# Order and bank flags of the output products in a decay attention with a feed-forward behind it

## The chip, the cores and the metric

The kernel runs on one core of a Trainium2 chip. The metric is the time of one execution on the device in microseconds (us). A core has five engines that run side by side and wait for each other by semaphores: TensorE (PE in the profile) multiplies matrices and writes into eight accumulator banks (PSUM), VectorE (DVE) and ScalarE (ACT) read those banks, GpSimd (POOL) works on the main on-chip memory alone, and SyncE (SP) issues the transfers.

## The reference

Eight heads of decayed linear attention over 4 batches of 768 tokens with head size 64, then a feed-forward layer with softplus:

```python
for t in range(S):
    state = gamma[None, :, None, None] * state + np.einsum('bhd,bhe->bhde', k[:, :, t], v[:, :, t])
    y[:, :, t] = scale * np.einsum('bhd,bhde->bhe', q[:, :, t], state)
...
x = np.ascontiguousarray(attn_out.transpose(0, 2, 1, 3)).reshape(B * S, H * D)
h = x @ w_in
g = np.maximum(h, 0.0) + np.log1p(np.exp(-np.abs(h)))
return (g @ w_out).astype(np.float32)
```

Here gamma differs by head; w_in is 512 by 2048, w_out 2048 by 512.

## The kernel before, in words

**Attention in units.** A unit is one chunk of 128 tokens for half of the heads (four heads): 4 batches of 6 chunks and 2 halves make 48. A unit passes through parts, one every few ticks: its loads (`load_unit`), the decay factors (`decay`, POOL), the operands (`operands`), the scores (`scores`), the new state (`new_state`), and the outputs with a copy of the state (`stack_and_outputs`). The state of earlier chunks stays summed in one bank (`stp`).

**Split operands.** PE multiplies in a reduced format (fp32r). The later units, those from number 12 on (WHOLE), therefore hold each operand as a high part and a low part: `kq` for keys and queries, `vhl` for values, `st` for the state, `ah` and `al` for the masked scores. Scores are made by PE two heads at a time (`sc`, L227), added up by DVE (L228), masked by POOL (L229), cast to `ah` by ACT (L233), and `al` is the difference, made by POOL (L234).

**The outputs.** For a later unit the outputs of its four heads lie in one tile `yp` of 64 partitions and 512 numbers, which fills one bank. Per head five products are summed there: state with the queries' high and low parts (L298, L299; not in a batch's first chunk, where there is no state), values' high part with `ah` (L300), values' high part with `al` (L301), values' low part with `ah` (L302). Then ACT casts them to `xh` (L304) and DVE takes the rest, `xl` (L306). Scores and outputs share the two banks of the pool `ps_a`.

**The feed-forward.** Blocks of 256 or 384 tokens go through 16 slices of the hidden size. A step makes one slice `hp` from `xh`, `xl` and the split first weights (L334 to L336, two banks in turn), then softplus in three steps on DVE and ACT (L341, L342, L346), a cast to `gh` (L348, ACT) and a rest `gl` (L350, POOL); two steps later the second product adds into `acc` (L365 to L367).

**What sets the order.** The code issues attention ticks between feed-forward steps by a plan. The order in which each engine then has its instructions comes from a scheduler that runs through the program with a modelled timeline: where an instruction's inputs are not there yet in its model, it puts a later instruction of the same engine that is ready ahead of it, and it picks the buffers of a pool along the way. On the chip every engine goes through its list strictly in that order.

Of the kernel before, what the change touches and what calls it, by code (L numbers as in the profile page):

```python
# [33 lines left out]
def decay_attention_then_softplus_ffn(ctx: ExitStack, tc: tile.TileContext, q, k, v, w_in, w_out, qtab, vtab, gtab, out):  # L34
    nc = tc.nc
# [8 lines left out]
    HH = H // 2  # L44
# [228 lines left out]
    def outputs(n):  # L273
        b, c, hf = units[n]
        kq, *rest, st = live.pop(n)
        off, g = places[n // 2], hf * NJ
        xh, xl = (x[:, g:g + NJ, off:off + C] for x in xring)
        if n < WHOLE:
            kn, vn, a = rest
            yp = ps_a.tile([P, NJ, C], F32, name="yp", tag="a")  # L280
            v0 = vns[n % 3].rearrange("p h t d -> p (h t) d")
            for j in range(NJ):
                if c:
                    nc.tensor.matmul(yp[:, j], lhsT=st[:, j, :], rhs=kq[:, j, :], start=True, stop=False)
                for par in range(2):
                    at = 2 * (2 * j + par) - par
                    nc.tensor.matmul(yp[:, j], lhsT=v0[:, at:at + 2, :], rhs=a[:, 2 * j + par, :], start=c == 0 and par == 0, stop=par == 1)
            nc.scalar.copy(xh, yp)
            nc.vector.tensor_tensor(xl, yp, xh.bitcast(F32), op=ALU.subtract)
            return  # L290
        yp = ps_a.tile([D, 2, NJ, C], F32, name="yp", tag="a")
        vhl, kn, vn, ah, al = rest
        for j in range(NJ):
            for par in range(2):
                h = 2 * j + par
                o = yp[:, par, j, :]
                if c:
                    nc.tensor.matmul(o, lhsT=st[:, par, j, :], rhs=kq[:, 1, par, j, :], start=True, stop=False)  # L298
                    nc.tensor.matmul(o, lhsT=st[:, par, j, :], rhs=kq[:, 2, par, j, :], start=False, stop=False)  # L299
                nc.tensor.matmul(o, lhsT=vhl[:, h, 0, :], rhs=ah[:, h, :], start=c == 0, stop=False)  # L300
                nc.tensor.matmul(o, lhsT=vhl[:, h, 0, :], rhs=al[:, h, :], start=False, stop=False)  # L301
                nc.tensor.matmul(o, lhsT=vhl[:, h, 1, :], rhs=ah[:, h, :], start=False, stop=True)  # L302
        for par, own, oth in sides:
            nc.scalar.copy(xh[own], yp[:, par])  # L304
        for par, own, oth in sides:
            nc.vector.tensor_tensor(xl[own], yp[:, par], xh[own].bitcast(F32), op=ALU.subtract)  # L306

    def stack_and_outputs(n):
        outputs(n)
        stack_state(n)  # L310
# [77 lines left out]
    for i, a, b in turns:  # L388
        m = WIDE // BLOCKS[i]
# [71 lines left out]
    for a, b in zip(starts, starts[1:]):  # L461
# [4 lines left out]
        for s in range(a, b):  # L466

            t, n = (s - a + 1, b - a) if i == 2 else (min(s - a, b - a - 2), b - a - 2)
# [59 lines left out]
```

## Time and profile before

| | |
|---|---|
| median of 3 runs | 686.2 us (682.22 to 686.45) |
| profiled execution | 683.14 us |
| its span, first to last instruction | 681.3 us |
| PE busy | 661.6 us (97%) |
| weight loads (PEld) busy | 600.3 us (88%) |
| DVE, ACT, POOL busy | 436.1, 358.0, 316.5 us |
| granted clock of PE | 0.997 |

Durations are those of the profiled execution. PE's matmuls overlap each other: one is shown from its start to its modelled end, and the next starts long before that end, so what a matmul costs in a dense stream is the step from start to start. Weight loads have rows of their own (PEld) and run beside the matmuls. A view that names a wait gives the idle time of an engine just before an instruction and what came last of that which it waited for.

### The profile page before, as it was taken

How to read it: one execution, taken by the hardware profiler on the slowest of the kernel's cores; microseconds unless marked ns; L12 is line 12 of the kernel's file. 1: busy time of each engine (PE TensorE's matmuls, PEld its weight loads, DVE VectorE, ACT ScalarE, POOL GpSimd, SP SyncE). 2: the span in 40 equal slices, each digit the busy share in tenths (PEclk: the TensorE clock that was granted, in tenths of full speed). 3: DMA queues.
4: the chain of work that ended last, by engine and by line, in shares of the span. 5: the costliest groups of instructions: out<-in, count | busy, mean ns of one | idle time of the engine just before them, and what ended most of it. 6: DMA issues, size and time to landing. Idle time of an engine off the chain costs nothing.

```text
span 681.3 us, 12857 instructions
## 1 busy us (share of the span) xinstructions
PE 661.6 (97%) x4146; PEld 600.3 (88%) x4146; DVE 436.1 (64%) x843; ACT 358.0 (53%) x808; POOL 316.5 (46%) x354
## 2 busy tenths in 40 slices
PE   7999899999999999999999999999999999999997
PEld 6898789988999999988999899988999899999996
DVE  5678698578567576785676766778666755432321
ACT  5788775545555355554555655455555545422221
POOL 5797666535435453454355344535344543332221
PEclk9999999999999999999999999999999999999999
DMA  9898653123112131222222222222212211000100
GB/s 246 237 270 231 184 141 72 26 69 82 35 36 53 29 95 26 40 39 64 48 38 54 37 77 42 37 36 53 76 37 38 36 33 47 1 1 1 46 1 32
DMA packets 153826, 46.75 MB, mean 69 GB/s; under 512 B 140448, under 2 KB 148640, under 8 KB 153760
## 3 DMA queue, kind: packets, MB, share of 16 engines
q1 hardware_dynamic: 153312, 45.93, 28.3%
q8 instruction: 33, 0.54, 0.3%
q14 instruction: 33, 0.27, 0.1%
q10 hardware_dynamic: 448, 0.01, 0.0%
HBM read 39.60 MB, written 6.29 MB: 67 GB/s over the span
## 4 chain that ended last, share of the span: by engine, by line
PE 52%; DVE 12%; SPq 11%; DMA 9%; issue 6%; ACT 5%; POOL 2%; DVEq 0%; ACTq 0%; POOLq 0%
SPq L136 10%; PE hp L334 8%; PE hp L336 8%; PE acc L365 8%; PE acc L367 8%; PE acc L366 8%; PE hp L335 8%; DVE kq L204 3%; DMA wout<-in_moe_w_out_dram 2%; DMA win<-in_moe_w_in_dram 2%; DMA kb<-in_k_dram 2%; DVE kq L208 2%; DMA qb<-in_q_dram 2%; DVE a L228 1%; DMA vn<-in_v_dram 1%
## 5 line engine op out<-in xcount | busy, mean ns | idle before, releaser
L350 POOL TENSOR_TENSOR gl<-sp,gh 128x384 fp32r<-128x384 f32 (+1 forms) x120 | 130.6, 1089 | 223.1 <-ACT gh L348 201.3
L334 PE MATMUL hp<-xh,winhl 128*128 128x384 f32 (+1 forms) x576 | 185.3, 322 | 2.4 <-DVE sp L346 1.9
L336 PE MATMUL hp<-xh,winhl 128*128 128x384 f32 (+1 forms) x576 | 184.7, 321 | 0.3 <-POOL winhl L99 0.3
L335 PE MATMUL hp<-xl,winhl 128*128 128x384 f32 (+1 forms) x576 | 183.7, 319 | 0.0
L365 PE MATMUL acc<-wouthl,gh 128*128 128x512 f32 x384 | 152.7, 398 | 0.0
L366 PE MATMUL acc<-wouthl,gh 128*128 128x512 f32 x384 | 151.8, 395 | 0.0
L367 PE MATMUL acc<-wouthl,gl 128*128 128x512 f32 x384 | 150.2, 395 | 0.0
L342 ACT ACTIVATE sp<-sp 128x384 f32<-128x384 f32 (+1 forms) x120 | 65.3, 546 | 137.7 <-DVE sp L341 134.6
L334 PEld LDWEIGHTS hp<-xh,winhl 128*128 128x128 f32 x576 | 108.8, 189 | 7.1 <-DVE sp L346 1.7
L335 PEld LDWEIGHTS hp<-xl,winhl 128*128 128x128 f32 x576 | 108.8, 189 | 3.7
L336 PEld LDWEIGHTS hp<-xh,winhl 128*128 128x128 f32 x576 | 108.7, 189 | 0.8 <-POOL winhl L99 0.5
L341 DVE TENSOR_SCALAR sp<-hp 128x384 uint32<-128x384 uint32 (+1 forms) x120 | 68.4, 573 | 61.1 <-PE hp L336 60.5
L348 ACT CAST gh<-sp 128x384 fp32r<-128x384 f32 (+1 forms) x120 | 64.1, 534 | 73.9 <-DVE sp L346 44.6
L346 DVE SCALAR_TENSOR_TENSOR sp<-hp,sp 128x384 f32<-128x384 f32 (+1 forms) x120 | 69.4, 580 | 34.6 <-ACT sp L342 33.6
L367 PEld LDWEIGHTS acc<-wouthl,gl 128*128 128x128 f32 x384 | 71.7, 188 | 14.4
L366 PEld LDWEIGHTS acc<-wouthl,gh 128*128 128x128 f32 x384 | 72.3, 188 | 11.1
L365 PEld LDWEIGHTS acc<-wouthl,gh 128*128 128x128 f32 x384 | 72.2, 188 | 10.9
L229 POOL TENSOR_SCALAR_AFFINE_SELECT a<-a 128x512 f32<-128x512 f32 x48 | 35.9, 749 | 48.5 <-DVE a L228 34.9
L228 DVE TENSOR_REDUCE a<-sc 128x256 f32<-128x512 f32 x72 | 48.9, 680 | 9.3 <-PE sc L227 7.8
L234 POOL TENSOR_TENSOR al<-a,ah 128x512 fp32r<-128x512 f32 x36 | 48.1, 1337 | 10.7 <-ACT ah L233 10.5
L204 DVE TENSOR_TENSOR kq<-kb,kq 64x256 fp32r<-64x256 f32 x72 | 49.7, 690 | 3.2 <-ACT kq L203 1.1
L199 DVE STREAM_TRANSPOSE kb<-kb 128x256 f32<-128x256 f32 x36 | 16.0, 445 | 51.8 <-DMA kb<-in_k_dram 39.8
(83 smaller groups left out, 994.0 us busy)
## 6 DMA issues: line engine op xcount, KB each, us to landing
win<-in_moe_w_in_dram SPq DMA_DIRECT2D x16, 512.0 KB, 4.5
wout<-in_moe_w_out_dram SPq DMA_DIRECT2D x16, 512.0 KB, 4.5
vn<-in_v_dram SPq DMA_DIRECT2D x48, 128.0 KB, 2.8
out_dram<-o SPq DMA_DIRECT2D x24, 256.0 KB, 2.1
kb<-in_k_dram SPq DMA_DIRECT2D x288, 16.0 KB, 1.7
qb<-in_q_dram SPq DMA_DIRECT2D x288, 16.0 KB, 1.7
vn<-in_k_dram SPq DMA_DIRECT2D x30, 128.0 KB, 2.4
qn<-in_q_dram SPq DMA_DIRECT2D x12, 128.0 KB, 4.7
```

The lines of the kernel that those rows point to most:

```text
L136: nc.sync.dma_start(t[at:at + 32, h // 2], src[b, hf * HH + h, c * C:(c + 1) * C, d:d + 32].rearrange("(i t) d -> t i d", t=32))
L204: nc.vector.tensor_tensor(kq[oth, 0, par], kt[own], kq[own, 0, par].bitcast(F32), op=ALU.subtract)
L334: nc.tensor.matmul(hp[:, k], lhsT=wt[:, 0, d, :], rhs=xh[:, d, :], start=d == 0, stop=False)
L335: nc.tensor.matmul(hp[:, k], lhsT=wt[:, 0, d, :], rhs=xl[:, d, :], start=False, stop=False)
L336: nc.tensor.matmul(hp[:, k], lhsT=wt[:, 1, d, :], rhs=xh[:, d, :], start=False, stop=d == ND - 1)
L341: nc.vector.tensor_scalar(sp.bitcast(U32), hps[s].bitcast(U32), 0x80000000, None, op0=ALU.bitwise_or)
L342: nc.scalar.activation(sp, sp, AF.Softplus)
L346: nc.vector.scalar_tensor_tensor(g, hps.pop(s), 0.0, g, op0=ALU.max, op1=ALU.add)
L350: nc.gpsimd.tensor_tensor(gl, sps.pop(s), gh.bitcast(F32), op=ALU.subtract)
L365: nc.tensor.matmul(acc[i][t], lhsT=gh[:, k, ts], rhs=wt[:, 0], start=begins and k == 0, stop=False)
L366: nc.tensor.matmul(acc[i][t], lhsT=gh[:, k, ts], rhs=wt[:, 1], start=False, stop=False)
L367: nc.tensor.matmul(acc[i][t], lhsT=gl[:, k, ts], rhs=wt[:, 0], start=False, stop=ends and f == fs[-1])
```

## The change

The products of a later unit's outputs are the same, in another order. Per head the new code issues the state products and the two products with `ah`; when all four heads have had theirs, it issues the four products with `al`. [...] Now only the very first matmul into the bank clears; all others add where something has been written since, and overwrite where nothing has. All have to come after that first one, which a dependency without a semaphore states.

```diff
--- before.py
+++ after.py
@@ -290,16 +290,27 @@
             return
         yp = ps_a.tile([D, 2, NJ, C], F32, name="yp", tag="a")
         vhl, kn, vn, ah, al = rest
+        opened = []
+
+
+        def into(o, l, r):
+            m = nc.tensor.matmul(o, lhsT=l, rhs=r, start=not opened, stop=True, skip_group_check=True)
+            if opened:
+                tc.add_manual_dep(m.ins, opened[0].name, mybir.DependencyInfo(mybir.DependencyClass.NoSync, mybir.DependencyReason.DATA), reason="the bank's first")
+            else:
+                opened.append(m.ins)
+
         for j in range(NJ):
             for par in range(2):
                 h = 2 * j + par
-                o = yp[:, par, j, :]
+                products = [(vhl[:, h, 0, :], ah[:, h, :]), (vhl[:, h, 1, :], ah[:, h, :])]
                 if c:
-                    nc.tensor.matmul(o, lhsT=st[:, par, j, :], rhs=kq[:, 1, par, j, :], start=True, stop=False)
-                    nc.tensor.matmul(o, lhsT=st[:, par, j, :], rhs=kq[:, 2, par, j, :], start=False, stop=False)
-                nc.tensor.matmul(o, lhsT=vhl[:, h, 0, :], rhs=ah[:, h, :], start=c == 0, stop=False)
-                nc.tensor.matmul(o, lhsT=vhl[:, h, 0, :], rhs=al[:, h, :], start=False, stop=False)
-                nc.tensor.matmul(o, lhsT=vhl[:, h, 1, :], rhs=ah[:, h, :], start=False, stop=True)
+                    products = [(st[:, par, j, :], kq[:, t, par, j, :]) for t in (1, 2)] + products
+                for l, r in products:
+                    into(yp[:, par, j, :], l, r)
+
+        for h in range(HH):
+            into(yp[:, h % 2, h // 2, :], vhl[:, h, 0, :], al[:, h, :])
         for par, own, oth in sides:
             nc.scalar.copy(xh[own], yp[:, par])
         for par, own, oth in sides:
```

In the new code all these products have one line, L297. Lines behind the change are numbered 11 higher than before (L334 is now L345, L341 is L352, L365 is L376).

PE, the run of the unit whose tile is `yp_4546`, from its first product with `ah`; `sc_4629` are the next unit's scores, `hp` and `acc` the feed-forward. Before:

```order
L227 MATMUL sc_4629<-kq1_85 128x256 x2
L300 MATMUL yp_4546<-ah_4474,vhl_4370 64x128
L365 MATMUL acc0_3971<-wouthl_901,gh_4495 128x512
L366 MATMUL acc0_3971<-wouthl_901,gh_4495 128x512
L367 MATMUL acc0_3971<-wouthl_901,gl_4497 128x512
L365 MATMUL acc1_3972<-wouthl_901,gh_4495 128x512
L366 MATMUL acc1_3972<-wouthl_901,gh_4495 128x512
L367 MATMUL acc1_3972<-wouthl_901,gl_4497 128x512
L365 MATMUL acc2_3973<-wouthl_901,gh_4495 128x512
L301 MATMUL yp_4546<-al_4475,vhl_4370 64x128
L302 MATMUL yp_4546<-ah_4474,vhl_4370 64x128
```

Now (the products of the last head with the state and `ah`, then what follows; those of the first three heads stand just ahead):

```order
L297 MATMUL yp_4546<-kq0_84,st0_4264 64x128 x2
L297 MATMUL yp_4546<-ah_4474,vhl_4370 64x128 x2
L297 MATMUL yp_4546<-al_4475,vhl_4370 64x128 x4
L346 MATMUL hp_4585<-xl_83,winhl_1122 128x384
L347 MATMUL hp_4585<-xh_82,winhl_1122 128x384
L345 MATMUL hp_4585<-xh_82,winhl_1122 128x384
L346 MATMUL hp_4585<-xl_83,winhl_1122 128x384
L347 MATMUL hp_4585<-xh_82,winhl_1122 128x384
L227 MATMUL sc_4629<-kq1_85 128x256 x2
```

Seven `acc` matmuls stood between the first product with `ah` and the first with `al`; now the other `yp` products stand there, and five `hp` matmuls and the next unit's scores, which were ahead of the run, come behind it.

PE, the unit `yp_3716` of a batch's first chunk (no state products). Before:

```order
L366 MATMUL acc0_3012<-wouthl_1131,gh_3620 128x512
L300 MATMUL yp_3716<-ah_3656,vhl_3548 64x128
L227 MATMUL sc_3782<-kq0_84 128x256 x2
L367 MATMUL acc0_3012<-wouthl_1131,gl_3622 128x512
L365 MATMUL acc1_3013<-wouthl_1131,gh_3620 128x512
L366 MATMUL acc1_3013<-wouthl_1131,gh_3620 128x512
L367 MATMUL acc1_3013<-wouthl_1131,gl_3622 128x512
L365 MATMUL acc2_3014<-wouthl_1131,gh_3620 128x512
L366 MATMUL acc2_3014<-wouthl_1131,gh_3620 128x512
L301 MATMUL yp_3716<-al_3657,vhl_3548 64x128
```

Now:

```order
L378 MATMUL acc2_3014<-wouthl_1131,gl_3622 128x512
L249 MATMUL stp_93<-vn2_92 128x128
L297 MATMUL yp_3716<-ah_3656,vhl_3548 64x128 x8
L297 MATMUL yp_3716<-al_3657,vhl_3548 64x128 x4
L227 MATMUL sc_3782<-kq0_84 128x256 x2
L249 MATMUL stp_93<-vn2_92 128x128
L345 MATMUL hp_3806<-xh_82,winhl_1336 128x384
L346 MATMUL hp_3806<-xl_83,winhl_1336 128x384
```

The run has moved behind the whole `acc` step and is in one piece, with the scores behind it.

DVE, between the second step of softplus of slice `sp_4538` and the scores' second reduce of the unit after `yp_4546` (`sc_4633`); `kb_4749` is a block of keys from a transfer. Before:

```order
L346 SCALAR_TENSOR_TENSOR sp_4538<-hp_4525,sp_4538 128x384
L341 TENSOR_SCALAR sp_4598<-hp_4585 128x384
L199 STREAM_TRANSPOSE kb_4749<-kb_4749 128x256
L228 TENSOR_REDUCE a_4628<-sc_4629 128x256
L346 SCALAR_TENSOR_TENSOR sp_4598<-hp_4585,sp_4598 128x384
L208 TENSOR_TENSOR kq0_84<-qb_4451,kq0_84 64x256
L228 TENSOR_REDUCE a_4628<-sc_4633 128x256
L208 TENSOR_TENSOR kq0_84<-qb_4451,kq0_84 64x256
L271 TENSOR_TENSOR st0_4571<-stp_93,st0_4571 64x128 x2
```

Now:

```order
L357 SCALAR_TENSOR_TENSOR sp_4538<-hp_4525,sp_4538 128x384
L199 STREAM_TRANSPOSE kb_4749<-kb_4749 128x256
L208 TENSOR_TENSOR kq0_84<-qb_4451,kq0_84 64x256 x2
L271 TENSOR_TENSOR st0_4571<-stp_93,st0_4571 64x128 x2
L352 TENSOR_SCALAR sp_4598<-hp_4585 128x384
L228 TENSOR_REDUCE a_4628<-sc_4629 128x256
L317 TENSOR_TENSOR xl_83<-yp_4546,xh_82 64x2x128 x2
L212 TENSOR_TENSOR vhl_4686<-vn2_92,vhl_4686 128x4x64
L357 SCALAR_TENSOR_TENSOR sp_4598<-hp_4585,sp_4598 128x384
L352 TENSOR_SCALAR sp_4666<-hp_4653 128x384
L228 TENSOR_REDUCE a_4628<-sc_4633 128x256
```

The transpose of `kb_4749` now stands ahead of a step of softplus (`sp_4598`) and of the differences for `kq0` and `st0`; between it and the second reduce stand eight rows where there were three.

## The prediction

> **What bounds the kernel now.** I read the page first: the busy times, then TensorE's (PE's) waits, then its timeline around the products that the change reorders. The later units (36 of the 48, those whose outputs come from split operands) run from about 130 to 623 us, and the changed lines lie in that stretch alone.
>
> The page's first part, busy time and share of the span by engine:
>
> ```profile
> PE 661.6 (97%) x4146; PEld 600.3 (88%) x4146; DVE 436.1 (64%) x843; ACT 358.0 (53%) x808; POOL 316.5 (46%) x354
> ```
>
> The windows view of that stretch (length, then busy time of PE, PE's weight loads, DVE, ScalarE and POOL, the clock):
>
> ```profile
> 130.00:623.00 493.00, 487.50 (x3005) 442.16 (x3004) 323.89 (x638) 252.77 (x599) 214.18 (x232) 1.00 0.21 44
> ```
>
> PE's waits in it (in total, times, longest):
>
> ```profile
> PE sc L227 <- DVE a L228: 3.8, 5, 1.5
> PE yp L301 <- POOL al L234: 1.0, 1, 1.0
> PE yp L300 <- ACT ah L233: 0.4, 1, 0.4
> PE hp L334 <- DVE sp L346: 0.3, 1, 0.3
> ```
>
> PE is busy 487.5 of 493 us, at full clock: only 5.5 us of idle time lie where the change works. 1.4 of them belong to the edited products (a wait for `al`, one for `ah`), 3.8 to the scores `sc`, which wait until VectorE (DVE) has read the scores before them.
>
> A busy PE also loses time that is no idle time. The timeline of PE (start, duration, line) around a unit of a batch's first chunk:
>
> ```profile
> 301.90 0.40 PE L366 MATMUL acc<-wouthl,gh 128*128 128x512 f32 x1
> 302.74 0.28 PE L300 MATMUL yp<-ah,vhl 128*64 128x128 f32 x1 [0.44 <-ACT ah L233]
> ...
> 304.06 0.39 PE L365 MATMUL acc<-wouthl,gh 128*128 128x512 f32 x1
> 304.29 0.39 PE L366 MATMUL acc<-wouthl,gh 128*128 128x512 f32 x1
> 304.52 0.22 PE L301 MATMUL yp<-al,vhl 128*64 128x128 f32 x1
> 304.58 0.22 PE L302 MATMUL yp<-ah,vhl 128*64 128x128 f32 x1
> ...
> 305.12 0.22 PE L302 MATMUL yp<-ah,vhl 128*64 128x128 f32 x1
> 305.18 0.44 PE L367 MATMUL acc<-wouthl,gl 128*128 128x512 f32 x1
> 305.46 0.60 PE L249 MATMUL stp<-vn 128*128 128x128 f32 x4
> ```
>
> Matmuls overlap, so the step from start to start is the price. `acc` steps by 0.23 us (304.06 to 304.29), `yp` by 0.06 (304.52 to 304.58) though each lasts 0.22. After a run of `yp` the first wide matmul takes 0.28 until the next start (305.18 to 305.46): 0.05 more than 0.23. The weight loads show why:
>
> ```profile
> L365 PEld LDWEIGHTS acc<-wouthl,gh 128*128 128x128 f32 x384 | 72.2, 188 | 10.9
> L301 PEld LDWEIGHTS yp<-al,vhl 128*64 128x64 f32 x144 | 19.5, 135 | 2.3 <-POOL al L234 1.6
> ```
>
> A wide load lasts 188 ns, a narrow one 135: the 53 ns more find too little cover under a `yp` of 60. So a return from a run of `yp` to wide work costs about 0.055 us.
>
> **The change, part by part.**
>
> *Nothing is removed or added in work.* Of PE's groups of later `yp` products (count, busy time, mean in ns) there are three with 144 and two with 120:
>
> ```profile
> L301 PE MATMUL yp<-al,vhl 128*64 128x128 f32 x144 | 31.3, 223 | 1.0 <-POOL al L234 1.0
> ...
> L299 PE MATMUL yp<-kq,st 128*64 128x128 f32 x120 | 26.7, 223 | 0.0
> ```
>
> The change issues the same 672 in the same shapes; clearing the bank once is a flag, not an instruction. At 0.06 us they take 40 us before and after: 0.
>
> *(a) Fewer runs.* In PE's order the later units' `yp` products form 85 runs before and 58 after, because the old chain broke at each unit's first `al` and the new one does not. 27 returns × 0.055 = **-1.5 us**. Bounds: 0 (the load is late at the seam all the same) and -1.5.
>
> The Trainium skill ("TensorE: Matmul & The Clock Gate", Back-to-back issue gap) gives about 81 ns per matmul for a sustained stream of load and matmul pairs at 128 columns moving. By it each of the 27 joined products would lose 21 ns and (a) would be -0.9 (an estimate from that page); this trace's runs step by 60, so the row decides.
>
> *(b) The wait for the low parts.* `al` is made on GpSimd (POOL) from `ah`:
>
> ```profile
> L234 POOL TENSOR_TENSOR al<-a,ah 128x512 fp32r<-128x512 f32 x36 | 48.1, 1337 | 10.7 <-ACT ah L233 10.5
> ```
>
> It ends about 1.4 us after `ah` at the earliest (1.34 and some 0.08 of handing over). Before, the scheduler put `acc` or `hp` work between a unit's first `ah` product and its first `al` product. Now the first `al` product comes 14 `yp` products (0.84 us) after the first `ah` product, 8 (0.48 us) in a batch's first chunk. Where PE comes to `ah` less than 0.6 us (0.9) after it is ready, it will wait for `al`. Behind a waiting PE stand the wide matmuls, and behind those the `sp` and `gh` steps of DVE and ScalarE, so a wait here moves everything. One place, on three engines:
>
> ```profile
> 371.52 0.62 ACT L233 CAST ah<-a 128x512 fp32r<-128x512 f32 x1 [1.99 <-POOL a L229]
> ...
> 372.00 0.33 PE L335 MATMUL hp<-xl,winhl 128*128 128x384 f32 x1
> ...
> 372.17 0.33 PE L336 MATMUL hp<-xh,winhl 128*128 128x384 f32 x1
> 372.22 1.30 POOL L234 TENSOR_TENSOR al<-a,ah 128x512 fp32r<-128x512 f32 x1 [0.15 <-ACT ah L233]
> 372.35 0.40 PE L227 MATMUL sc<-kq 128*128 128x256 f32 x2
> 372.58 0.22 PE L300 MATMUL yp<-ah,vhl 128*64 128x128 f32 x1
> ...
> 374.31 0.22 PE L301 MATMUL yp<-al,vhl 128*64 128x128 f32 x1
> ```
>
> Now `ah` is ready at 372.14, PE uses it at 372.58, and 7 `acc` matmuls cover `al` (ready 373.52). In the new order five `hp` (0.17 each) and a pair of `sc` (0.24) that stood ahead of the run stand behind it, 1.1 us of work: PE arrives at 371.5, waits 0.7 for `ah`, and after 14 products 0.5 for `al`: 1.2. The same pattern returns two blocks later, in the unit ahead of the 538.71 quoted in (c), with 1.0. The unit at 302.74 now has all its `acc` ahead, arrives 1.8 us later and finds both ready, unless its scores come later, (c): 0 to 1.8, I take 0.7. I went through the other 33 in the same way: none waits over 0.4. New waits 2.9, against 1.7 gone (0.98 and 0.44 of idle, with some 0.16 each until the pipe is full: 301.90 + 0.23 to 302.74 is 0.61): **+1.2 us**. Bounds: -1.7 (none left) and +5 (twice those found).
>
> *(c) The scores.* The score and `yp` tiles share two banks, so where `yp` ends decides when scores start, and the scheduler has moved DVE's rows along. The largest stall, on PE and DVE:
>
> ```profile
> 375.33 0.44 PE L366 MATMUL acc<-wouthl,gh 128*128 128x512 f32 x1
> ...
> 376.24 0.45 DVE L199 STREAM_TRANSPOSE kb<-kb 128x256 f32<-128x256 f32 x1 [2.62 <-DMA kb<-in_k_dram]
> ...
> 376.60 0.65 DVE L228 TENSOR_REDUCE a<-sc 128x256 f32<-128x512 f32 x1
> ...
> 377.31 0.50 PE L227 MATMUL sc<-kq 128*128 128x256 f32 x2 [1.54 <-DVE a L228]
> ```
>
> Its twin two blocks later, on PE:
>
> ```profile
> 538.71 0.50 PE L227 MATMUL sc<-kq 128*128 128x256 f32 x2 [0.97 <-DVE a L228]
> ```
>
> And a smaller one, on PE, with the transpose that follows it on DVE:
>
> ```profile
> 295.03 0.51 PE L227 MATMUL sc<-kq 128*128 128x256 f32 x2 [0.47 <-DVE a L228]
> ```
>
> ```profile
> 296.09 0.45 DVE L199 STREAM_TRANSPOSE kb<-kb 128x256 f32<-128x256 f32 x1 [1.11 <-DMA qb<-in_q_dram]
> ```
>
> At 373.6 DVE stands still for a transpose whose block of k has not landed; the reduce behind it holds PE. In the new order 12 `hp`, a ninth `acc` and a state product stand ahead of these scores, and DVE has the transpose, two `kq` differences, two of the state, one `sp` and then the reduce. From these rows:
>
> ```profile
> 377.64 0.40 DVE L208 TENSOR_TENSOR kq<-qb,kq 64x256 fp32r<-64x256 f32 x1
> ...
> 379.12 0.59 DVE L271 TENSOR_TENSOR st<-stp,st 64x128 fp32r<-64x128 f32 x2
> ...
> 382.03 0.55 DVE L341 TENSOR_SCALAR sp<-hp 128x384 uint32<-128x384 uint32 x1
> ```
>
> the reduce would end at 376.6 + 0.8 + 0.6 + 0.55 + 0.68 = 379.2, and PE arrives at about 379.5: the 1.75 us are gone, and so are the 1.2 of its twin at 538.71. At 295 it goes the other way: the transpose, which stood behind the first reduce, now stands ahead of it. Landing at 296.1, with 0.45 + 0.55 + 0.68 the reduce ends at 297.7; PE, with 1.7 us more work ahead, comes at 296.1 and waits 1.6 where it waited 0.6. The other two change by 0.3 or less. Of 4.9 us (3.8 idle, five restarts) I take **-2.0**. Bounds: -4.9 (none left) and +4.9 (as many anew), since DVE has more such pauses than reach PE:
>
> ```profile
> DVE kb L199 <- DMA kb<-in_k_dram: 39.8, 23, 4.4
> ```
>
> *(d) Behind the run.* Each unit's first high-part cast (`xh`, ScalarE) needs heads 0 and 2. They were complete five products before the run's end, now two: 0.18 us later against the end, while the run itself ends earlier in most units. Only two of 36 units have ScalarE idle for it:
>
> ```profile
> ACT xh L304 <- PE yp L302: 4.0, 2, 2.0
> ```
>
> At 53% busy ScalarE hides it: 0; without that cover 36 × 0.18 = 6.5 us, on ScalarE and not on PE. The skill ("Perfetto Trace Analysis", Optimizing Tensor Performance) wants independent groups in different banks, so that emptying one overlaps the next group's matmuls. That speaks against finishing four heads together; by it the sum would be up to 6.5 higher, and the row says that little of it is real. SP's and POOL's queues get no new instruction; some loads swap places in SP's, and what that can do is inside (c).
>
> **Sum**: -1.5 + 1.2 - 2.0 = -2.3 us. The profiled execution took 683.1 us (span 681.3 and 1.8 around it), so 680.8; it ran 3.1 below the median of 686.2, itself one of 682.2 to 686.5. Against the median I forecast 686.2 - 2.3 = **684 us**.
>
> **The rivals.**
>
> *All waits go.* The earlier ends free the banks everywhere: -1.5 - 1.7 - 4.9 - 0.4 = -8.5, or 678 us. For it: the stalls sit where runs were torn apart. Against: DVE's pauses come from late blocks of k, which the edit does not touch.
>
> *The low parts are uncovered.* If waits pile up upstream and PE meets `ah` as soon as it is cast, each unit waits 1.4 - 0.84 = 0.56 (30 units) or 0.9 (six): 16.8 + 5.4 = 22 us, about 706: slower. It decides from the point where PE comes to `ah` within 0.6 us of its end. Today 3 of the 36 pairs of rows like those at 371.52 and 372.58 are that close and most are 1.5 to 4 us apart, while the scheduler moved no run's start ahead by more than 1.8; so `ah` itself would have to become late.
>
> *DVE's pauses spread.* With the transpose ahead of the reduce in more units, as at 295, PE meets as many stalls again: +4.9 - 0.3 = about +4.6, or 691 us.
>
> *It does nothing.* If (a) to (c) cancel: 686.
>
> **How the numbers follow.** About 1% (7 us) is what a measurement of this kernel can tell from no change. Chances: the forecast, 680 to 688 (doing nothing is in it), 0.65; all waits go 0.12; pauses spread 0.16; low parts uncovered 0.07. Range: 678 to 691 takes in the forecast and most of the two neighbours, and leaves out the uncovered case and half of the first rival. Faster by over 1% is most of the first rival: 0.11. Slower by over 1% is the uncovered case and a rest of the third: 0.09. Within: 0.80.
>
> **What would show it.** PE's groups: the single line of all 672 `yp` products with a mean near 223 ns, steps of 0.06 and idle of 2 to 4 us put down to `al` and `ah`. PE's waits: `sc` on the reduce at 1 to 3 us, gone near 377 and 539, larger near 296. Return steps unchanged at 0.28. The windows view: PE idle 4 to 6 us between 130 and 623. The prediction is wrong if `yp` idle passes 6 us, if the mean `yp` step leaves 0.06, or if a wait that is not there now (`hp` on `sp`, `acc` on `gl`) holds PE for over 3 us.

## The result, and the profile after

The changed kernel takes 694.64 us (median of four runs, 689.91 to 697.22), the kernel before 684.21 beside it: a ratio of 1.0154, 95% interval 1.012 to 1.0188. It is slower by 1.5%, where 684 us and a range of 678 to 691 had been predicted. The profiled execution took 696.13 us, its span is 694.1 at a mean clock of 0.998.

The page's busy times of the changed kernel:

```profile
PE 663.6 (96%) x4146; PEld 600.0 (86%) x4146; DVE 432.9 (62%) x843; ACT 357.9 (52%) x808; POOL 315.7 (45%) x354
```

The windows view of the same 493 us as before the change (length, then PE, weight loads, DVE, ScalarE, POOL, clock):

```profile
130.00:623.00 493.00, 477.75 (x2922) 431.29 (x2922) 316.47 (x631) 247.65 (x589) 208.40 (x228) 1.00 0.21 44
```

PE's waits in it:

```profile
PE acc L376 <- DVE o L390: 6.0, 4, 3.4
PE yp L297 <- POOL al L234: 3.6, 8, 1.1
PE stp L249 <- DVE st L271: 1.5, 3, 0.7
PE hp L345 <- DVE sp L357: 1.3, 2, 0.9
PE yp L297 <- ACT ah L233: 1.1, 1, 1.1
PE sc L227 <- DVE xl L317: 0.9, 2, 0.6
PE sc L227 <- DVE a L228: 0.8, 3, 0.3
```

No engine has more instructions; PE stands still for 15.2 us there instead of 5.5. The scores' waits have mostly gone (3.8 to 1.7 us), as predicted. In first place is a wait that the page before did not have at all: `acc`, the first product of a new block, waits until DVE has copied the finished block's sums (`o`) out of the same bank.

Idle time leaves out the restart behind a wait. So the table counts each PE step (start to start) against the median step of its shape, from 130 us on, by what ended it; the sum of all differences is in the last row. It grows by 13.7 us, the span by 12.8.

| PE's step was ended late by | before | after |
|---|---|---|
| `o`, copies of finished blocks | 0 | 6.6 |
| `al` and `ah`, for `yp` | 1.7 | 6.7 |
| the reduce, for `sc` | 5.2 | 1.5 |
| `xl`, for `sc` | 0 | 1.2 |
| `st`, for `stp` | 0 | 2.0 |
| `sp`, for `hp` | 0.5 | 1.6 |
| all, with what is left | 13.5 | 27.2 |

The largest stall, on DVE, then SP, then PE of the changed kernel:

```profile
482.86 1.71 DVE L204 TENSOR_TENSOR kq<-kb,kq 64x256 fp32r<-64x256 f32 x2
...
486.66 0.55 DVE L352 TENSOR_SCALAR sp<-hp 128x384 uint32<-128x384 uint32 x1
489.89 0.45 DVE L199 STREAM_TRANSPOSE kb<-kb 128x256 f32<-128x256 f32 x1 [2.68 <-DMA kb<-in_k_dram]
490.26 0.65 DVE L390 COPY o<-acc 128x512 f32<-128x512 f32 x1
490.83 0.54 DVE L357 SCALAR_TENSOR_TENSOR sp<-hp,sp 128x384 f32<-128x384 f32 x1
495.34 0.69 DVE L390 COPY o<-acc 128x512 f32<-128x512 f32 x1 [3.97 <-DMA out_dram<-o]
```

```profile
484.59 3.65 SPq L136 DMA_DIRECT2D kb<-in_k_dram  x8
490.94 5.46 SPq L392 DMA_DIRECT2D out_dram<-o  x3
```

```profile
492.28 0.40 PE L378 MATMUL acc<-wouthl,gl 128*128 128x512 f32 x1
496.09 0.79 PE L376 MATMUL acc<-wouthl,gh 128*128 128x512 f32 x1 [3.41 <-DVE o L390]
...
497.95 0.52 PE L345 MATMUL hp<-xh,winhl 128*128 128x384 f32 x1
498.27 0.52 PE L346 MATMUL hp<-xl,winhl 128*128 128x384 f32 x1
```

Read it from the top. A block of k has two places. The second split of keys (L204) ends at 484.57 and frees one; at 484.59 SP begins the eight transfers of the next block. The last of them lands 1.7 us after its issue, and DVE's next instruction is the transpose of just that block: DVE stands for 2.68 us, with the copy of the finished block behind it. The third copy needs one of two output tiles and waits until the first has been written out. PE needs that bank at 492.5 and gets it at 496.09; behind it the `hp` steps are 0.32 us instead of 0.17. The two other long waits for copies, at 326.0 and 328.8, stand behind another such transpose, for which DVE waits 3.64 us. In all DVE waits longer for k than before (39.8):

```profile
DVE kb L199 <- DMA kb<-in_k_dram: 60.3, 24, 4.2
```

The same place before the change, on DVE and then SP:

```profile
473.73 1.19 DVE L204 TENSOR_TENSOR kq<-kb,kq 64x256 fp32r<-64x256 f32 x2
474.85 0.54 DVE L341 TENSOR_SCALAR sp<-hp 128x384 uint32<-128x384 uint32 x1
...
480.30 0.45 DVE L199 STREAM_TRANSPOSE kb<-kb 128x256 f32<-128x256 f32 x1 [1.84 <-DMA kb<-in_k_dram]
480.67 0.52 DVE L341 TENSOR_SCALAR sp<-hp 128x384 uint32<-128x384 uint32 x1
481.12 0.67 DVE L379 COPY o<-acc 128x512 f32<-128x512 f32 x1
...
484.01 0.69 DVE L379 COPY o<-acc 128x512 f32<-128x512 f32 x1 [1.67 <-DMA out_dram<-o]
```

```profile
474.95 3.71 SPq L136 DMA_DIRECT2D kb<-in_k_dram  x8
```

And the third bank's first product, on PE:

```profile
486.11 0.39 PE L365 MATMUL acc<-wouthl,gh 128*128 128x512 f32 x1
```

There DVE stood too, for 1.84 and 1.67 us, but PE came for the bank 1.4 us after the third copy had ended (484.01 + 0.69). The pause was there; the margin hid it. It was also shorter. In both kernels some 5.3 us lie between the first transfer of the block and its transpose (474.95 to 480.30, 484.59 to 489.89), but DVE had five instructions to do in between and now has three, so it comes to the transpose earlier and stands there longer.

### The profile page after: what moved, and what is told of

Its sections match the earlier page's. It is cut to its first block, busy times and chain, and to the rows that moved or that the text cites. A ratio compares the mean times of both kernels' runs of the same rounds, so it can differ in the third digit from the quotient of the medians.

```text
span 694.1 us, 12866 instructions
## 1 busy us (share of the span) xinstructions
PE 663.6 (96%) x4146; PEld 600.0 (86%) x4146; DVE 432.9 (62%) x843; ACT 357.9 (52%) x808; POOL 315.7 (45%) x354
## 4 chain that ended last, share of the span: by engine, by line
PE 52%; DMA 10%; SPq 10%; DVE 9%; issue 4%; ACT 4%; POOL 4%; DVEq 0%; POOLq 0%; ACTq 0%
SPq L136 10%; PE acc L377 8%; PE acc L376 8%; PE acc L378 8%; PE hp L345 8%; PE hp L347 8%; PE hp L346 7%; DMA kb<-in_k_dram 3%; PE yp L297 3%; DMA qb<-in_q_dram 3%; DVE kq L204 2%; DMA vn<-in_k_dram 2%; PE sc L227 2%; POOL al L234 1%; DMA out_dram<-o 1%
## 5 line engine op out<-in xcount | busy, mean ns | idle before, releaser
L345 PE MATMUL hp<-xh,winhl 128*128 128x384 f32 (+1 forms) x576 | 185.7, 323 | 3.6 <-DVE sp L357 3.1
L376 PE MATMUL acc<-wouthl,gh 128*128 128x512 f32 x384 | 152.6, 398 | 6.0 <-DVE o L390 6.0
L345 PEld LDWEIGHTS hp<-xh,winhl 128*128 128x128 f32 x576 | 109.1, 189 | 9.0 <-DVE sp L357 2.0
L352 DVE TENSOR_SCALAR sp<-hp 128x384 uint32<-128x384 uint32 (+1 forms) x120 | 68.6, 573 | 52.6 <-PE hp L347 51.9
L376 PEld LDWEIGHTS acc<-wouthl,gh 128*128 128x128 f32 x384 | 72.3, 188 | 17.7 <-DVE o L390 5.5
L199 DVE STREAM_TRANSPOSE kb<-kb 128x256 f32<-128x256 f32 x36 | 16.0, 444 | 71.9 <-DMA kb<-in_k_dram 60.3
L204 DVE TENSOR_TENSOR kq<-kb,kq 64x256 fp32r<-64x256 f32 x72 | 44.6, 620 | 2.7 <-ACT kq L203 0.4
```

What stands on the lines that cost most here:

```text
L345: nc.tensor.matmul(hp[:, k], lhsT=wt[:, 0, d, :], rhs=xh[:, d, :], start=d == 0, stop=False)
L352: nc.vector.tensor_scalar(sp.bitcast(U32), hps[s].bitcast(U32), 0x80000000, None, op0=ALU.bitwise_or)
L376: nc.tensor.matmul(acc[i][t], lhsT=gh[:, k, ts], rhs=wt[:, 0], start=begins and k == 0, stop=False)
```

## The experiments

**The theories.** *A, late keys:* blocks of k that land late hold DVE, and the copies (and whatever else PE needs from DVE) come late behind them. *B, low parts:* the waits for `al` are the loss. *C:* the flags, the bank cleared once. A later one, *F*, is on the output transfer in the stall above. Ratios are to the kernel before, run beside each.

**The parts of the change.** The flags alone, in the old order:

```diff
-                products = [(vhl[:, h, 0, :], ah[:, h, :]), (vhl[:, h, 1, :], ah[:, h, :])]
+                products = [(vhl[:, h, 0, :], ah[:, h, :]), (vhl[:, h, 0, :], al[:, h, :]), (vhl[:, h, 1, :], ah[:, h, :])]
...
-        for h in range(HH):
-            into(yp[:, h % 2, h // 2, :], vhl[:, h, 0, :], al[:, h, :])
```

> The old order of the products, with the bank cleared by its first matmul alone; every engine has its instructions in the old order. Three theories. (A, late keys) The new order moves VectorE's split of the keys behind softplus steps, so the next block of keys lands late, VectorE stands at its transpose and the copies of the finished block's outputs stand behind it; PE's acc waits for them. (B, low parts) The cost is PE waiting for al, which nothing covers now. (C, flags) Accumulating all products into a bank that is cleared once costs time by itself. A and B expect the time before, 684 us within 3; C expects about 694.

684.28 us, 0.9998 (0.9978 to 1.0018), with every engine's order that of the kernel before. C falls: the loss is the order's.

The new order in only some of the units, the old one in the rest (`c > 0` here; `c == 0` in the other run):

```diff
+                if not (c > 0):
+                    products.insert(1, (vhl[:, h, 0, :], al[:, h, :]))
...
-        for h in range(HH):
+        for h in range(HH if c > 0 else 0):
```

> The new order, but in the first chunk of each batch (6 of the 36 later units) a head's product with al stands between its two products with ah as before. In VectorE's list a fourth row comes back between the split of the keys and the transpose ahead of the copies at the two places where PE's acc waited longest (326 to 329 and 491 to 496 us of the changed kernel). A expects acc's wait to fall from 6.6 us to under 2 and the slow clock behind it to go: 685 to 689 us. B expects the waits for al in the other 30 units to stay, and 691 to 695.

688.37 us, 1.0066 (1.0043 to 1.0089): in A's range, and no wait for a copy, as A said; but 3.1 us go for `al` and 5.8 for the scores.

> The new order only in the six later units that begin a batch; the other thirty in the old order. With the new order in those thirty alone acc waited for no copy (688.4 us). Theory A (the first chunks' new order moves the split of the keys behind DVE's softplus steps, hence late keys and copies): acc waits 4 to 7 us for o, al under 2 us, 688 to 692. If the late copies need the new order in both kinds of units, or have to do with neither: acc waits under 1 us and 684 to 686.

695.64 us, 1.0154 (1.0125 to 1.0184): six units in the new order cost as much as all 36. PE's waits there, from 130 to 623 us:

```profile
PE sc L227 <- DVE a L228: 6.0, 6, 1.9
PE acc L378 <- DVE o L392: 2.7, 4, 1.1
PE yp L297 <- POOL al L234: 2.7, 5, 1.0
```

The wait for copies is back, smaller than A had it (2.7 us for 4 to 7); the time is above A's 688 to 692, since PE also waits 6.0 us for the scores and 2.7 for `al`. The loss does not go with the number of edited units; where everything else falls decides it.

**The copies.** All copies of finished blocks on ScalarE, and, apart from that, a third output tile (the places of `part` are free by then):

```diff
-                (nc.scalar.copy if t % 2 else nc.vector.tensor_copy)(o, acc[i][t])
+                nc.scalar.copy(o, acc[i][t])
```

> The changed kernel with the copies of a finished block's sums all on ScalarE instead of two of three on VectorE, so that none stands behind VectorE's transposes. PE's order is the changed kernel's but for 4 places. A expects acc's wait for the copies to go (6.6 us and some 2 us of slow clock): 685 to 688 us. B expects 693 to 696, no change.

691.59 us, 1.0099 (1.007 to 1.0128). PE's wait for the copies is down to 0.4 us, but its wait for `al` rises from 3.6 to 5.3: 3 us came back where 7 to 10 had been expected.

> The kernel before with all copies of finished blocks on ScalarE, DVE's order else but for some 27 rows the same: the control to the changed kernel with the same edit (691.6 us, 3 below the changed kernel, where 7 to 10 were expected). If the copies cost ScalarE nothing: 683 to 686. If they delay the cast ah and what hangs on it there too: 687 to 690, and the 3 us are what is left of some 6.

The control: 684.28 us, 0.9985 (0.9959 to 1.0012), nothing. So the edit is worth some 0.5% in the changed kernel and nothing that can be told in the other; the intervals do not quite keep the two apart.

```diff
-            o = ffn.tile([P, DM], F32, name="o", tag="o")
+            o = ffn.tile([P, DM], F32, name="o", tag="part" if t == 2 else "o")
```

> The changed kernel with a third place for output tiles (the third tile of a block goes to the unused place of an earlier buffer), so that the second copy on VectorE no longer waits for a transfer out to end (1.8 and 4.0 us there). The order is the changed kernel's but for 2 rows on VectorE and ScalarE. A expects the longer half of acc's wait to go and the slow clock with it: 687 to 691 us. B expects 693 to 696.

687.39 us, 1.0041 (1.0019 to 1.0064): over two thirds of the loss.

> The kernel before with a third output tile for a block's last rows: the control to the changed kernel with it. The kernel before has no wait of acc for o, so by theory A nothing: 683 to 685.5 us. If a third tile is worth something by itself (DVE's stalls at the copies, 8.7 us waiting for output transfers, hold the reduces behind them): 680 to 682.5, and the 7 us it is worth in the changed kernel are no measure of what the change cost there.

681.22 us, 0.9934 (0.9911 to 0.9957). This control changes the reading: the third tile is worth 0.7% without the change as well, and of the 1.1% that it gives back in the changed kernel only some 0.5% belong to the change, and the intervals hardly tell that from nothing. It is also a version that beats both kernels and leaves nothing out. With the tile in both, the change still costs 1.1% (1.0041 / 0.9934).

**The low parts.** The last four products take `ah` again; a dependence without a wait keeps the order:

```diff
...
-            into(yp[:, h % 2, h // 2, :], vhl[:, h, 0, :], al[:, h, :])
+            m = into(yp[:, h % 2, h // 2, :], vhl[:, h, 0, :], ah[:, h, :])
+            tc.add_manual_dep(m, al.name, ..., reason="order alone")
```

> The changed kernel, but a unit's last four products take the scores' high parts ah a second time in place of the low parts al (GpSimd still makes al, nobody reads it): the output lacks the low parts' share, and no product waits for al. By start-to-start steps the changed kernel's products lose 5.1 us to al beyond 130 us, 1.1 in the kernel before. Theory B (a wait for al is time lost): 694.6 - 5 = 689 to 691 us, with the wait of acc for o still at some 6 us. Theory A (late keys hold DVE's copies of finished blocks, and that alone sets the time; whoever arrives earlier waits there longer): 693 to 696 us. Something else than both: below 687.

687.97 us, 1.007 (1.0047 to 1.0093): some 6 us back, as B said and a little more, for the wait of `acc` for copies fell as well, from 6.0 to 2.5.

> The changed kernel with the third output tile (687.4 us by itself) and, as in the run before, the last four products of a unit taking ah in place of al, so that the output lacks the low parts' share; the order on the engines is that of the kernel with the third output tile but for a few neighbours. That kernel's steps lose 3.7 us to al. Theory A and B together (two losses that add up): 683 to 685 us, the kernel before's time. Theory A alone: 686.5 to 688.5, since PE would meet other waits instead.

686.09 us, 1.0029 (1.0012 to 1.0047). With the third tile alone 1.0041: the two do not add up, and the time falls between the two forecasts. Each gives back 6 to 8 us alone, both together 8 to 9. They are not two losses side by side.

The low products a step of the schedule later:

```diff
-    PARTS = {-6: load_unit, -2: decay, 0: operands, 2: scores, 3: new_state, 5: stack_and_outputs}
+    PARTS = {-6: load_unit, -2: decay, 0: operands, 2: scores, 3: new_state, 4: high_outputs, 5: stack_and_outputs}
...
```

> The changed kernel with a unit's high products one step of the schedule earlier than its four low products and casts, so that GpSimd has time to make al. Theory B: PE waits for al under 1 us in all, and if the late copies stay, 688 to 691; the order also frees the keys' buffers otherwise, which can take the copies' wait with it: 684 to 687. Rival: the outputs' bank is held longer, and the scores that want it wait: sc loses over 8 us by steps and the time is 692 to 700.

691.87 us, 1.0072 (1.0045 to 1.01). PE still waits 2.3 us for `al`, and 2.2 for `st`, 1.8 for `xl`. The waits are spread over other names; neither side of the expectation is met.

**A third place for the blocks of k.**

```diff
-        t = attn.tile([P, NJ, C // 32, 32], F32, name=f"{nm[0]}b", tag=nm, bufs=2)
+        t = attn.tile([P, NJ, C // 32, 32], F32, name=f"{nm[0]}b", tag=nm, bufs=3 if nm == "kn" else 2)
...
```

> The changed kernel with a third buffer for a block of k, loaded and transposed, so that its load need not wait until DVE has split the keys before (the identity matrix takes a place of the tag al before its first use). Theory A (late keys): DVE's wait for k, 60.3 us, falls under 30, PE's wait of acc for o (6.0) under 1, and the time to 685 to 689 us, the rest being the waits for al. If the copies are late for another reason, the output transfers ahead of them or ScalarE's and DVE's own work: acc still waits over 4 us for o, 692 to 696.

> The kernel before with the third buffer for a block of k: what that buffer is worth without the change. The kernel before loses 5.2 us by steps at scores that wait for DVE's reduce behind a late transpose. Theory A: DVE's wait for k (39.8 us) falls under 20 and the time by 1 to 4 us, 681 to 684. If late keys don't reach PE in the kernel before: 684 to 686.

695.39 us, 1.0183 (1.0154 to 1.0213), and 692.27, 1.0121 (1.0093 to 1.0149): nothing gained in the one, 1.2% lost in the other, where A had expected a gain in both. DVE's wait for k did not fall (61.9 and 41.2 us for 60.3 and 39.8). The edit did not take away what it was to take away, so it says nothing for or against A. The reason was found in the trace of the next pair, in which k and q both have three places, with nearly the order of the two kernels:

```diff
+        n = 2 * (b * NC + c) + hf
+        pool, tag = (ffn, "part") if n > 18 and n % 3 == 2 else (attn, nm)
-        t = attn.tile([P, NJ, C // 32, 32], F32, name=f"{nm[0]}b", tag=nm, bufs=2)
+        t = pool.tile([P, NJ, C // 32, 32], F32, name=f"{nm[0]}b", tag=tag, bufs=2)
```

> The changed kernel with three places for the blocks of k and three for those of q from the nineteenth unit on: SP need not wait for the splits of the unit before last. Theory A (late blocks are the common cause): DVE's wait for k (60.3 us) falls under 25, PE's waits for the copies and for al under 2 us together, and the time to 677 to 683 us, below the kernel before. If the 280 transfers less were what counted, or SP's issuing (8 transfers in 3.65 us) is what makes keys late: DVE's wait for k stays over 45 us and the time at 688 to 696.

> The kernel before with the same third places: the control. Theory A: its stalls of scores behind late transposes go, 680 to 684 us, so that the changed order is the faster of the two by some 2 to 5 us, as with one block of k for all (678.3 against 683.9). If the two orders then cost the same, the change's own gain of fewer returns from narrow to wide products is not there: within 1.5 us of each other.

690.26 us, 1.0056 (1.0039 to 1.0072), and 689.92, 1.0053 (1.0029 to 1.0078). The two orders now cost the same, both lose to the kernel before, and both miss what A had expected. DVE's wait for k with three places, in the changed order, from 130 to 623 us:

```profile
DVE kb L201 <- DMA kb<-in_k_dram: 50.6, 20, 4.3
```

By the expectation these numbers (over 45 us, 688 to 696) are those of A's rival, by which SP's eight transfers for a block are what makes keys late, or by which having 280 transfers fewer (in the runs of the next part) is what counts. Counting blocks in the traces gives another reason. In the changed kernel a block's load begins 0.03 us (median) after the split of the block before last, its transpose 0.28 us after it has landed, and its own split 19 us after the transpose: the block turned at 489.89 is split at 517.36. With three places the load begins 0.03 us after the split of the block one further back, the transpose is again 0.28 us behind the landing, and the split 31 us behind the transpose. The scheduler puts the transpose into DVE's order where the block arrives in its model, however long before anybody needs it. A further place moves the load and the transpose ahead together, and DVE goes on standing at transposes whose result nobody waits for. So the run does not take the lateness away either, and it decides nothing between A and the rival.

**Keys that cannot be late.** One block of k for all later units, loaded once, transposed for each:

```diff
-        for x in rest:
-            blocks = x.rearrange("p m i d -> p (m i d)")
-            nc.vector.transpose(blocks, blocks)
+        rest = [attn.tile([P, NJ, C // 32, 32], F32, name="kb", tag="kn", bufs=2), rest[1]]
+        for x, y in zip(rest, (kept[0], rest[1])):
+            nc.vector.transpose(x.rearrange("p m i d -> p (m i d)"), y.rearrange("p m i d -> p (m i d)"))
...
```

> The changed kernel with one block of k for all later units, loaded once and transposed for each unit as before: the output is that of wrong keys, the loads of k for the other 35 units (280 of SP's transfers) are left out, and no unit's keys can be late. PE's order is the changed kernel's but for its first fifth. Theory A (late keys hold DVE, behind it the copies of finished blocks): DVE waits 0 for k, PE under 1.5 us for copies, the slow steps at 497 are gone, and the time is 685 to 688 us, 4 to 5 us of waits for al being left; if the low parts too are late through late blocks, 683 to 685. Rival (the load of q, next in SP's queue, or DVE's own row of work holds the copies as long): acc still waits over 4 us for o, 691 to 696.

678.33 us, 0.9907 (0.9882 to 0.9933), better than A had it. The windows view, from 130 to 623 us:

```profile
130.00:623.00 493.00, 493.00 (x3068) 451.58 (x3067) 326.10 (x648) 259.87 (x608) 217.61 (x237) 1.00 0.16 36
```

PE does not wait once in 493 us: not for a copy, not for `al`, not for scores, states or softplus. By the table's count 3.4 us are lost instead of 27.2. POOL's wait for blocks of q, which the 280 missing transfers could have helped, did not fall, from 26.2 in the changed kernel:

```profile
POOL qb L184 <- DMA qb<-in_q_dram: 29.6, 17, 3.8
```

The order is nearly that of the changed kernel: behind 200 us PE's differs in 24 of 2898 places and DVE's, without the transposes of k, in 26 of 543. The transposes themselves stand elsewhere.

> The kernel with one block of k for all, and besides the last four products of a unit with ah in place of al (wrong keys, no low parts of the scores in the output); its order is that of the run before. If late keys and waits for al are all that the change cost: 680 to 683 us, like the kernel before with the same edit to its keys, and by start-to-start steps under 13 us lost beyond 130. If something else costs as much (hidden products that wait for sp, states that wait for st): 685 to 688.

677.63 us, 0.9902 (0.9879 to 0.9925): without the low parts nothing more is gained. In this order, with the keys on time, `al` is on time.

> The kernel before with one block of k for all later units (wrong keys, 280 transfers left out): the control to the two runs ahead of it. Theory A: its scores' stalls behind late transposes (5.2 us by steps) go, 679 to 682 us. If late keys cost the kernel before nothing: 683 to 685.

683.92 us, 0.9978 (0.9962 to 0.9994), where A had 679 to 682: by the time, late keys cost the kernel before next to nothing. By the table's count it does lose less beyond 130 us (some 9 us instead of 13.5; the scores' stalls are gone), but both runs lose 4 to 5 us more than the two kernels ahead of 130 us, and why is open. Waits are left there (1.4 us of `hp` for `sp`, 0.9 of `yp` for `ah`, 0.5 in others), and the run with the changed order is the faster one by 0.7% (0.9907 / 0.9978). The control is not quite the old order: behind 200 us PE's differs from that of the kernel before in 504 of 2893 places.

That the new waits go when no block of k can be late is shown by this pair, as far as runs can show it that leave out 280 of SP's transfers with the lateness and move the transposes. That each wait hangs on a late block is not shown: the state's wait at 538.7 stands behind a transpose of q, at which DVE waited 1.84 us for POOL. How late keys on DVE come to hold `al`, which POOL makes, was not followed link by link and stays argued. To order each transpose behind the split of the block before, which would leave the loads a unit's time, was not tried.

**The instruction transfer beside the output (F).** In the stall at 490.94 two output transfers land after 4.3 and 4.4 us, where 2.1 is usual. The transfers from 490.9 to 495.3 us of the changed kernel, by queue:

```profile
q8 instruction: 1, 0.02, 2.4%
...
out_dram<-o SPq DMA_DIRECT2D x2, 256.0 KB, 4.4
```

One packet of instructions takes 2.4% of 16 engines' 4.4 us, which is 1.7 us of one engine. The page counts 33 of them, 16 KB each, so one in some 21 us:

```profile
q8 instruction: 33, 0.54, 0.3%
```

With 128 instructions more on PE at the start they come half a period earlier:

```diff
-    for _ in range(5):
-        nc.tensor.matmul(warm, lhsT=stw[0][:, 0, :], rhs=stw[0][:, 0, :], start=True, stop=True)
+    for _ in range(37):
+        nc.tensor.matmul(warm[:, :8], lhsT=stw[0][:, 0, :], rhs=stw[0][:, 0, :8], start=True, stop=True)
```

> The changed kernel with 37 matmuls of 8 columns in place of the five of 128 that warm TensorE up at the very start: 128 instructions more on that engine, whose instruction transfers of 16 KB (256 instructions, one each 21 us) so come half a period earlier. The order after some 200 us is the changed kernel's. In the changed kernel such a transfer begins at 492.0, beside two output transfers issued at 490.9 and 491.4, which land after 4.3 us where 2.1 is usual, and the third copy of that block and PE wait for them (3.4 us, after which PE's steps are slow for 3 us). Theory F (the instruction transfer holds one DMA engine): the two land after 2.1 to 2.3 us, PE's longest wait of acc for o falls to 1.0 to 1.6, and 3 to 4 us of the 10 come back, 690 to 692. If the landing is late for another reason (the weights' or keys' loads) it stays at 4 us and the time at 693 to 697.

703.84 us, 1.0261 (1.0237 to 1.0286). The time was missed by far: the edit also rearranged the first 200 us, and the first output is issued at 153.28 instead of 139.71; why is open. The stall itself did what F said. The two transfers land after 2.1 and 2.3 us, and PE's longest wait for a copy is 1.2, from 158 to 636 us:

```profile
PE acc L376 <- DVE o L390: 2.7, 3, 1.2
```

From the issue of the first output to that of the last this run takes 546.0 us, the changed kernel 551.3, the kernel before 537.3. It differs in more than the packets, but the parts agree: 2.2 us of late landing and 1.6 of slow steps, some 4 us of the loss, hang on a collision at a place where DVE's copy, and behind it PE, waited for the output tile. The kernel before met such landings too (3.7 us for an output issued at 565.4), but at the last output of a block, whose tile nobody was waiting for.

## Why the prediction was wrong

**(a) Fewer runs** was right. The products come back to wide work 58 times instead of 85, at a median of 0.054 us more each: 4.8 us before, 3.5 after, -1.3 for -1.5 predicted. The steps of `yp` stayed at 0.06; the 81 ns of the Trainium skill ("TensorE: Matmul & The Clock Gate", Back-to-back issue gap) do not show in this trace.

**(c) The scores** was right in sum: -2.0 predicted, 5.2 to 1.5 by steps, or -2.5 with the new wait for `xl`. The stalls at 377.31 and 538.71 are gone, as worked out; the one at 295 is gone too, where 1.6 us had been expected. So the sum came out partly by luck: the 1.6 did not come, and 1.2 for `xl` came that had no term.

**(d) Behind the run** was right; ScalarE's wait of `xh` for the run went from 4.0 to 1.3 us.

**(b) The wait for low parts** was mis-sized. The three units worked out came true: the one at 372 waits 0.8 us (at 378.2), its twin 1.2 (at 548.4), the one at 302.74 waits 0.4 (at 307.6), by steps 2.5 for 2.9. But of the 1.7 us counted as gone 1.2 stayed (the first of these waits is now for `ah`), and "none waits over 0.4" failed for four other units by 0.05 to 0.2, while eight small waits make 3.0 us together: +5.0 for +1.2, the upper bound. Two things were left out. The interval from the end of `ah` to its first product, 2.6 us in the median of the units before, shrank to 1.6, since PE comes to the runs earlier against the rest. And `al` does not begin when `ah` ends: in nine units POOL was at something else for another 0.8 us or more (three before). One of them, on ScalarE, POOL and PE of the changed kernel:

```profile
458.30 0.62 ACT L233 CAST ah<-a 128x512 fp32r<-128x512 f32 x1
...
458.53 1.20 POOL L361 TENSOR_TENSOR gl<-sp,gh 128x384 fp32r<-128x384 f32 x1
459.69 0.80 POOL L180 TENSOR_TENSOR vn<-vn,vtabs 128x256 f32<-128x256 f32 x1
460.45 1.28 POOL L234 TENSOR_TENSOR al<-a,ah 128x512 fp32r<-128x512 f32 x1
...
461.78 0.46 PE L297 MATMUL yp<-al,vhl 128*64 128x128 f32 x4 [0.46 <-POOL al L234]
```

`ah` ends at 458.92; with POOL free, `al` would have been ready at 460.3, and PE would not have waited.

**The step that failed** is the path in (c): it lets DVE's pauses reach PE through the reduce alone ("since DVE has more such pauses than reach PE"). DVE has more in its order that PE needs. The copies of finished blocks (0 to 6.6 us, and 1.6 more in slow steps), the state (0 to 2.0) and softplus (0.5 to 1.6) were in no term. With (a), (b) and (c) at their measured sizes the sum would have been -1.3 + 5.0 - 2.5 = +1.2, some 687 us and inside the range; the missing terms make 6.6 + 1.6 + 2.0 + 1.1 = 11.3 us of the 13.7. The copies stood in the trace of before, at the place shown, with a margin of 1.4 us. And the prediction had taken DVE's 39.8 us of waiting for k as given; they became 60.3.

**The rivals.** "DVE's pauses spread" was the right kind at half the size, by another door: it priced the reduce at +4.6 and did not think of the copies. "The low parts are uncovered" did not come: PE met `ah` within 0.6 us of its end in six units instead of three. "All waits go", 678 us, is about what the order does when keys cannot be late (678.3); that the two numbers agree so well is luck, since that run leaves out 280 transfers and loses more ahead of 130 us. Its counter-argument was half right: the pauses come from late blocks, but the edit did touch them. Of the signs named, the last one, "a wait that is not there now", was the one to come, with another name than the two given; PE's idle time, 15.2 us for the 4 to 6 named, was the other.

## What to carry to other kernels

An engine that goes through its list in order makes everything behind a late transfer late, and a reordering elsewhere decides what that is. So before one moves work, one lists for each pause of such an engine every instruction behind it on which the bound engine waits, with its margin; a margin of 1 to 2 us is no cover. Where a pause is at work that nobody needs yet, the place of that work in the order would be the thing to mend (not tried here); another buffer only sent it further ahead. And a fix is judged with its control: the third output tile gave back over two thirds of the loss, and more than half of that it gives the kernel before as well.

## What the runs showed of the hardware

**A transfer of instructions delays an output.** In the 20 traces of this study there are 480 output transfers of 256 KB. For 43 of them one of the 16 KB instruction packets begins in the 1.5 us behind their issue: all 43 land after 2.4 to 4.5 us. The median of the others is 2.1; 48 of them also take 2.4 or more, so that such a packet is not the only cause. But for all 31 that take over 3.2 us a packet begins between 0.1 us ahead of the issue and 2.5 us behind it. The run that moved the packets bears it out at one place. The Trainium skill ("DMA: Bandwidth & Descriptors", Queues, rings and completion order) says that a DMA engine changes between queues only at the end of a whole packet; if an output is spread over all engines, it then waits for the one that is busy, which would agree with these landings. On which engine a packet ran no trace here shows.

**The clock can halve behind a single stall.** The windows view of the changed kernel around the 3.41 us of idle time (length, then busy time of PE, weight loads, DVE, ScalarE, POOL, and the clock):

```profile
492.30:496.09 3.79, 0.38 (x3) 0.00 (x1) 0.75 (x2) 0.81 (x2) 0.76 (x1) 1.00 0.25 93
496.10:499.40 3.30, 3.30 (x10) 3.01 (x11) 2.96 (x8) 2.77 (x8) 0.00 (x0) 0.50 0.24 84
499.60:503.00 3.40, 3.40 (x21) 3.10 (x20) 2.43 (x4) 0.53 (x1) 1.01 (x1) 1.00 0.19 30
```

The granted clock is 0.50 for 3.3 us: here a stall of 3.4 us costs 1.6 more. The Trainium skill ("TensorE: Matmul & The Clock Gate", Part 1: The HAM clock gate) gives half rate after an idle window of about 3.4 us and full rate after a busy one as long; both numbers agree with this trace. The other traces show that much less idle time can do it. The windows view of the kernel before with three places (`c16_before_three_deep`), where PE is idle for 1.91 of 3.41 us:

```profile
377.91:381.32 3.41, 1.50 (x9) 1.29 (x9) 2.40 (x5) 3.26 (x10) 0.00 (x0) 1.00 0.03 5
381.32:384.73 3.41, 3.41 (x12) 3.21 (x11) 3.26 (x8) 1.16 (x3) 3.02 (x3) 0.50 0.14 23
```

Between 20 us and the last 5 us of the 20 traces the clock is halved 19 times, mostly for 3.41 us, and in the 3.41 us ahead PE is idle for 1.5 to 3.4. And a stall as long as the one above can go without: in the changed kernel with one block of k, PE is idle from 80.79 to 84.24 us, and the clock stays:

```profile
80.79:84.24 3.45, 0.00 (x0) 0.00 (x1) 3.33 (x8) 3.40 (x9) 0.00 (x0) 1.00 0.53 137
84.24:87.65 3.41, 3.41 (x29) 3.41 (x30) 3.34 (x7) 3.10 (x7) 2.87 (x3) 1.00 0.79 210
```

The changes of the clock lie whole multiples of 3.41 us apart, so one can count these stretches on through a trace: this stall falls into two of them, with 1.7 and 1.8 us each. So how a stall falls across these stretches, and not its length alone, seems to decide whether it costs half a stretch more. Stretches with 1.5 to 1.8 us of idle time occur with the half clock behind them and without it.
